# Prefix sums of four chunks as 64x64 tiles from three exact bf16 parts, with row 1's sums swapped between partition halves, and new orders of the whole program

## The chip, the cores and the metric

The kernel runs on one core of one Trainium2 chip. TensorE (PE) multiplies matrices into PSUM, VectorE (DVE) and ScalarE (ACT) work element by element, GpSimd (POOL) does slower element work and issues DMAs by software, and SyncE (SP) here only issues DMAs. Each engine takes its instructions strictly in order. The metric is the device time of one execution in microseconds. Before the change the median of three runs is 196.53 us (195.69 to 196.65).

## The reference

A gated linear attention is followed by a bilinear feed-forward layer. Batch 4, 8 heads, 768 positions, head size 48; the model width is 8 x 48 = 384 and the hidden width 1536.

```python
for t in range(S):
    state = alpha[:, :, t, :, None] * state + einsum('bhd,bhe->bhde', k[:, :, t], v[:, :, t])
    y[:, :, t] = einsum('bhd,bhde->bhe', q[:, :, t], state)
x = y.transpose(0, 2, 1, 3).reshape(B * S, H * D)
out = (x @ w_a) * (x @ w_b) @ w_out
```

The kernel does the recurrence in blocks. Within a block the decays are products of alpha, so it takes the logarithm of alpha, adds up along the positions (the prefix sums of this case), and scales q by exp(sum) and k by exp(-sum). Then masked scores q k^T times v give the part inside a block, and a state of 48x48 per head carries the rest over.

## The kernel before

**Chunks.** There are six chunks. Chunk c holds the two batch rows `2*(c%2)` and `2*(c%2)+1` (called u = 0 and 1 below, "row 0" and "row 1") and the 256 positions number c//2. A partition holds two successive positions, so 128 partitions hold 256 positions of a row. They are split at partition 64 into two halves (g = 0 and 1) of 128 positions each, and the prefix sums start anew in each half. Chunks 2, 3, 4, 5 are the ones that the change is about; chunk 0 sums every position by itself (`cum_both`, L588 and L589), and chunk 1 goes on as it was.

**The order.** Nothing is scheduled by the compiler: `PROGRAM` (L17 to L405) lists all operations of all chunks in one sequence, as `chunk: op args; op args`, and each engine gets its own instructions in that order. A number at the end of a PE operation is the PSUM bank (8 banks, L449). The letters V, S, P, Y at the end of others name VectorE, ScalarE, GpSimd and SyncE's DMA queue.

**One chunk.** `ld` loads alpha, k, q, v (L547). `ln` takes the logarithm (ACT, L554). `l2` adds the two positions of a partition (DVE, L561). The prefix sum is a product with an upper triangular matrix of ones, in which the block between the two halves is zero. The fast fp32 form of the product (type fp32r) rounds its input, so the sum to be multiplied is first split: `H` makes the rounded part `lh` (ACT L596 or DVE L598), `L` the remainder `ll` (DVE, L604), and `A2` multiplies both with the 128x128 triangle `utr`, two matmuls of 384 columns for one batch row (L628). `E` takes exp of plus and minus the sums (ACT, L656), `mk` and `mq` multiply k and q with them into `QKp` (DVE, L666); before that `lv` brings the first position of a pair to the level of the second (L642, on POOL or DVE; `ra` on ACT, L635, prepares a factor). `dr` and `dl` (SP, L671 and L676) carry the last sum of each half through DRAM into the column form `bl` that the state needs. `T` transposes `QKp` by DMA on SP (L718) in chunks 2 to 5; chunks 0 and 1 transpose on PE (`C`, L707, and `Ce`, L713 or L715) and take the decay from PE and ACT (`dk` L687, `de` L692).

**Attention and state.** `K` multiplies keys with values (L744), `k` updates the state (DVE, L758, L761, L762; it reads `bl`), `D` makes scores (L773), `M` or `Mc` then `Mm` masks them (L778; L782 on ACT and L786 on DVE), `SB`, `SA` and `Y` add up the output in PSUM (all L797), `X` takes it out as `xT` (L832, L834). `K`, `D`, `SB`, `SA`, `Y` use PE as four 64x64 tiles at once: four matmuls on different row and column halves of the array run side by side. In all of them the two row halves write different PSUM banks at any one time.

**Feed-forward.** `a` and `b` multiply `xT` with a 128-column piece of w_a and w_b (three matmuls each, L851; 512 columns for `*`, 256 for one row), `as` copies a (ACT, L857), `pr` multiplies (DVE, L865), `o` and `oc` are the last product (six matmuls of 384 or 192 columns, L873 and L884), `ot` takes it out (L888, L890), `st` stores it (SP, L906). All of these use the array whole, 128x128. In `PROGRAM` the feed-forward of a chunk is spread between the attention steps of the next ones, and so PE has work while the other engines prepare.

**The start.** `fill 7 6` (L571) runs seven matmuls on zeros while the first alpha is loaded.

Of the kernel before, what the change touches and what calls it, by code (L numbers as in the profile page):

```python
# [17 lines left out]
0: ld a 0b Y; cm 0; cz 0 q P; cz 0 b P; c1; cs 0 m V; c1a; ld a 0a Y; ld k 0b Y; ld q 0b Y; cu; ld q 0a Y; fill 7 6; cu2 P; ld v 0 P; cus; ld a 1 P; ln 0b  # L18
0: B 0b 5; ln 0a; ci; ld q 1 P; B 0a 0; E 0b i; E 0b b; ld k 0a Y; cz 1 b P; ld k 1 P; dk 0 3; mk 0b V; mq 0b V; E 0a b; C 0 1 4; cm 1; ld v 1 P; E 0a i
0: mq 0a V; W b 0 256; fill 3 1; mk 0a V; Ce 0 1 S; C 0 0 0; v 0 V; de 0; D 0 1 6; Ce 0 0 V; K 0 0 5; k 0 0 V; W a 0 256; M 0 1; D 0 0 4; SB 0 0; ln 1; W a 256 768  # L20
0: cz 0 v V; W b 256 768; M 0 0; B 1a 2
1: ld a 0 P
0: cs 1 0 P
1: ld a 1 P
0: B 1b 6; E 1a i; E 1a b; mq 1a V; mk 1a V; W a 768 1536; dk 1 5; E 1b i; C 1 0 2; de 1; v 1 S; mk 1b V; SA 0; Y 0; Ce 1 0 V; W b 768 1536; D 1 0 3
1: ld k 0 P
0: E 1b b; K 1 0 5; cs 1 m V; mq 1b V; X 0 S
1: ld v 0 P
0: K 0 1 2; C 1 1 6; a 0 0 0; a 1 0 7; Mc 1 0; k 0 1 V; Ce 1 1 V; k 1 0 V; a 2 0 3; as 1 0
1: ld q 0 P  # L30
0: cs 0 0 P; b 1 0 1; D 1 1 6; as 0 0; SB 1 4; Mm 1 0 V; as 2 0; Mc 1 1; a 3 0 0; pr 1 0; a 4 0 2; c2 P; Wo 0 6; cz 1 q V; Wo 6 12; b 2 0 3; pr 2 0; Mm 1 1 V
0: as 3 0; b 0 0 6; b 4 0 1; b 5 0 7; pr 0 0; Y 1; SA 1; K 1 1 6
1: ln 0
0: as 4 0
1: l2 0 V; ld k 1 P
0: X 1 S; b 3 0 0; a 5 0 2
1: ln 1
0: a 5 1 4; a 4 1 5; pr 3 0; pr 4 0; as 5 0; a 3 1 0; b 5 1 3
1: l2 1 V
0: pr 5 0; as 4 1; b 4 1 2; as 5 1; a 1 1 5; b 1 1 1; pr 4 1  # L40
1: ld q 1 P
0: cz 1 v P
2: ld a * P
0: as 1 1; a 6 * 4; as 3 1; pr 1 1
1: ra 0
0: a 0 1 0; a 2 1 7; a 8 * 1; b 3 1 2; pr 5 1; k 1 1 V
1: H 1 V; H 0 S
0: as 6 *
1: L 1 V
0: b 2 1 3; a 11 * 5; pr 3 1  # L50
1: L 0 V
0: a 7 * 6
1: ld v 1 P
0: as 11 *; b 6 * 2; as 2 1; pr 6 *; b 11 * 7; a 10 * 4
1: ra 1
0: as 0 1; pr 2 1
1: v 0 V
0: pr 11 *; as 7 *
1: lv 0 k P; A2 0 2
2: ld k * P  # L60
0: b 0 1 0
1: A2 1 5
0: as 8 *; b 7 * 3
1: lv 0 q V
0: pr 0 1
2: ld q * P
1: E 1 i; E 0 b
0: pr 7 *
1: E 1 b; E 0 i; mq 0 V
0: b 10 * 6; b 9 * 1; a 9 * 7; as 9 *; as 10 *  # L70
1: mk 0 V
0: b 8 * 0
1: dk * 5
0: pr 8 *; pr 10 *; pr 9 *
1: C 0 1 3; C 0 0 4
0: o 3 0 0
1: Ce 0 1 S; de *; Ce 0 0 V; K 0 0 7; D 0 0 4; k 0 0 V; K 0 1 3; D 0 1 1; Mc 0 0; lv 1 k P; SB 0 6; M 0 1
0: o 3 1 -
1: mk 1 V
0: o 0 0 5; ot 3 S  # L80
2: ln *
1: lv 1 q V
2: ld v * P
3: ld a * P
0: o 0 1 -
1: mq 1 V
0: o 2 0 4
1: Mm 0 0 V; k 0 1 V; C 1 0 2
0: o 1 0 0
1: Ce 1 0 V; v 1 V  # L90
2: l2 * V
0: ot 0 S; o 1 1 -
2: ra 0
1: SA 0
0: ot 1 S
2: H * S
1: D 1 0 1; K 1 0 3
2: lv 0 k P
1: M 1 0; Y 0
0: o 2 1 -  # L100
1: X 0 S; C 1 1 5
0: ot 2 S
1: a 5 0 6
2: L * V
1: Ce 1 1 V
2: lv 1 k P
1: a 3 0 1; k 1 0 V; as 3 0; a 1 0 0; as 5 0; b 1 0 7; b 3 0 2; as 1 0
2: A2 1 1
1: pr 3 0
2: ra 1  # L110
3: ld k * P
1: pr 1 0; SB 1 5
2: E 1 i
1: D 1 1 3; K 1 1 2; M 1 1
2: lv 1 q P; lv 0 q P; E 1 b
1: a 11 0 0
2: A2 0 7
1: as 11 0; b 11 0 1
2: E 0 i
1: b 5 0 0; pr 11 0  # L120
2: E 0 b
1: a 4 0 4; pr 5 0; a 0 0 3
2: dr
1: a 6 0 1; k 1 1 V; as 4 0; as 0 0; a 2 0 0; b 4 0 7
2: mk 1 V
1: as 6 0; b 6 0 3; pr 6 0; a 7 0 1; b 0 0 2; pr 4 0; b 7 0 4; pr 0 0; a 9 0 3; as 9 0
2: mq 1 V
1: as 2 0; SA 1; Y 1; as 7 0
2: T 1
1: b 9 0 2; X 1 S; pr 7 0; a 8 0 3; pr 9 0; b 2 0 0; as 8 0  # L130
2: v 1 S
1: b 8 0 1; pr 2 0; a 10 0 4; b 10 0 2
3: lv 0 k P
1: a 0 1 0
2: mq 0 V
1: as 10 0; a 9 1 5; as 0 1; pr 10 0; a 5 1 6
4: ld a * P
1: b 5 1 7
3: ln *
1: b 0 1 3; pr 8 0; a 2 1 0  # L140
2: dl
3: lv 1 k P
1: as 5 1; pr 0 1; a 1 1 2; b 1 1 4; as 1 1; pr 5 1; as 9 1; b 9 1 3; pr 1 1; as 2 1; a 8 1 6
2: mk 0 V
1: a 4 1 7; b 2 1 1
2: v 0 S
1: as 4 1; pr 9 1; a 11 1 2; b 11 1 0; b 4 1 5; pr 2 1; b 8 1 3; pr 4 1; as 8 1; pr 8 1
3: l2 * V
1: a 3 1 4
2: T 0  # L150
1: as 11 1; a 7 1 1; b 3 1 6
0: st 3 Y
1: o 2 0 5; a 10 1 7; as 7 1
3: ld q * Y
1: pr 11 1; as 3 1
0: st 1 Y
1: as 10 1; pr 3 1
2: D 1 0 3; K * 0 1; Mc 1 0; D 1 1 6; k * 0 V
1: a 6 1 0; b 7 1 2
3: ra 1  # L160
2: Mc 1 1
1: pr 7 1
5: ld a * Y
1: b 10 1 3; o 2 1 -; as 6 1
3: ra 0
0: st 0 Y
1: b 6 1 4; ot 2 S; pr 10 1
2: Mm 1 0 V; D 0 0 2; K * 1 1
3: H * V
1: pr 6 1; o 3 0 0  # L170
2: Mc 0 0; k * 1 V; Mm 1 1 V; SB 0 4; SB 1 6
3: L * V
2: D 0 1 2
3: lv 1 q P
1: o 0 0 1
2: Mc 0 1
1: o 3 1 -
2: Mm 0 0 V
4: ln *
3: A2 1 3  # L180
2: Mm 0 1 V; SA 1
3: ld v * P
4: ld v * P
2: Y 1; Y 0; X 1 V; SA 0
3: A2 0 2
2: X 0 S
3: E 0 b
1: o 0 1 -
3: lv 0 q V; E 1 b; E 0 i; mk 0 V
1: ot 3 S  # L190
3: E 1 i
2: b 5 * 6; b 3 * 4; a 4 * 5; a 5 * 7
1: ot 0 S
3: mq 1 V
2: a 3 * 2; a 2 * 1
3: dr
2: a 1 * 3; as 5 *; b 0 * 7; as 3 *; b 1 * 0; as 1 *
3: v 1 V
2: pr 5 *; pr 3 *; as 2 *
1: st 0 Y; st 3 Y  # L200
4: ld q * P
3: dl
2: b 2 * 3
3: mq 0 V
2: a 6 * 1
3: T 0
0: st 2 Y
2: as 6 *; pr 1 *
4: l2 * V; H * V; ra 1
2: as 4 *; b 4 * 2; a 11 * 0; b 6 * 6; a 0 * 4; b 8 * 1  # L210
1: o 1 0 5
4: L * V
2: pr 2 *; pr 6 *
3: v 0 V
2: as 0 *; a 8 * 3; pr 4 *; as 11 *; pr 0 *
3: mk 1 V
2: b 11 * 2; a 7 * 6; as 8 *; pr 11 *
1: o 1 1 -
2: pr 8 *
3: T 1  # L220
1: st 2 Y
3: K * 0 2
1: ot 1 S
3: k * 0 V
4: ld k * Y
1: st 1 Y
3: K * 1 0; D 0 0 3
2: as 7 *
3: Mc 0 0
2: b 9 * 1  # L230
3: k * 1 V
2: a 9 * 7
5: ld k * Y
2: b 10 * 5; as 9 *; a 10 * 6; b 7 * 3; pr 9 *; as 10 *; o 0 0 0; pr 7 *; pr 10 *
3: D 1 1 6; D 1 0 1
4: lv 1 k P
3: M 1 1
2: o 0 1 -
3: Mc 1 0
5: ld q * P  # L240
3: Mm 1 0 V; SB 0 3
2: ot 0 S
3: SB 1 1; D 0 1 5
4: lv 1 q V; A2 0 0
2: o 2 0 7
3: Mc 0 1
4: ra 0; lv 0 k V
5: ln *
4: E 0 b
3: Mm 0 1 V  # L250
2: o 3 0 6
3: Mm 0 0 V
5: lv 1 k P
4: lv 0 q P
5: ld v * P
3: Y 1; SA 0; Y 0; SA 1
2: o 3 1 -
3: X 0 S; X 1 V
2: o 2 1 -
4: mq 0 V; A2 1 2  # L260
2: ot 2 S
3: a 2 * 5
5: l2 * V
3: b 4 * 3
4: E 1 b; E 0 i; E 1 i
3: b 3 * 4; a 4 * 7; b 2 * 2
4: v 1 S
3: as 2 *
4: dr
5: H * S  # L270
2: ot 3 S
5: ra 0
2: st 0 Y
4: mk 0 V
3: as 4 *
4: mk 1 V
2: st 2 Y
3: a 8 * 1
4: T 0
3: a 1 * 0; a 0 * 6; b 8 * 7; as 8 *; b 5 * 5; pr 2 *; pr 4 *  # L280
4: v 0 V; dl
5: lv 0 q V
3: pr 8 *
4: mq 1 V
5: lv 0 k V
3: as 0 *
5: ra 1
3: a 3 * 1; a 5 * 3; b 0 * 7; a 9 * 6; as 5 *; pr 5 *; a 7 * 3; a 11 * 5; pr 0 *; as 9 *; as 3 *; as 1 *
4: T 1
3: b 9 * 6; b 1 * 1  # L290
5: lv 1 q V
3: pr 9 *; a 6 * 2; pr 3 *; as 11 *; pr 1 *; as 6 *
4: K * 0 0; D 0 0 4
5: L * V
3: as 7 *; b 11 * 6; b 6 * 7; pr 11 *; a 10 * 1; pr 6 *
4: Mc 0 0
2: o 1 0 5
3: as 10 *
4: k * 0 V; D 1 0 3; D 1 1 6; D 0 1 1
5: v 1 S  # L300
4: Mc 1 0; M 1 1
5: A2 0 0
2: o 1 1 -
4: SB 0 6; Mc 0 1; Mm 0 0 V; SB 1 3
2: ot 1 V
5: A2 1 2
3: b 7 * 1
5: E 1 i; E 1 b; E 0 b
3: b 10 * 5
4: Mm 0 1 V; Mm 1 0 V  # L310
3: pr 7 *; o 1 0 2
5: mk 1 V
3: pr 10 *; o 2 0 1
5: mq 1 V
4: Y 1; SA 0
5: dr
2: st 3 Y
5: T 1
4: Y 0; SA 1; X 1 S
5: E 0 i  # L320
3: o 1 1 -; o 2 1 -
4: X 0 V
5: mk 0 V; mq 0 V
3: ot 1 S
4: a 6 * 0; a 7 * 5; as 6 *
5: T 0
4: b 6 * 3; as 7 *; a 1 * 6
5: dl
4: pr 6 *; a 0 * 5; b 7 * 7; pr 7 *
3: ot 2 V; st 1 Y  # L330
4: as 0 *; as 1 *; a 5 * 3; b 1 * 4; b 0 * 2
2: st 1 Y
3: st 2 Y
4: pr 1 *; as 5 *; pr 0 *
5: v 0 V
4: a 3 * 0; a 4 * 7; as 3 *
5: D 0 0 5
4: as 4 *
5: K * 0 4; M 0 0; D 1 1 2; D 1 0 0; Mc 1 1
3: o 3 0 7  # L340
5: k * 0 V; Mc 1 0
3: o 3 1 -
5: SB 1 5
3: ot 3 S
5: SB 0 3; D 0 1 0
4: b 10 * 2
3: o 0 0 7
5: M 0 1; Mm 1 0 V; Mm 1 1 V
4: b 3 * 1; b 4 * 0
3: o 0 1 -  # L350
4: pr 4 *; b 5 * 0
3: ot 0 S
5: SA 1
4: pr 5 *
5: Y 1; Y 0
4: pr 3 *
5: X 1 V; SA 0
4: a 2 * 7; a 10 * 6
5: X 0 S
4: as 10 *; as 2 *; a 8 * 5  # L360
5: a 4 * 3
4: b 2 * 0
3: st 0 Y
5: a 2 * 4
4: pr 2 *; as 8 *; a 9 * 7
5: b 2 * 1; a 11 * 0
4: pr 10 *; b 8 * 5
5: as 2 *; as 4 *; a 1 * 4
4: b 9 * 2; pr 8 *
5: pr 2 *; b 5 * 3; b 1 * 6  # L370
4: as 9 *
5: b 4 * 1; a 8 * 5
4: a 11 * 7
5: pr 4 *
4: pr 9 *
5: b 11 * 1; as 11 *; as 1 *; a 5 * 4; a 0 * 2; pr 11 *; pr 1 *; as 0 *; as 5 *; b 0 * 0; b 7 * 6
4: o 0 0 1; as 11 *
5: pr 5 *; pr 0 *; as 8 *; a 10 * 2
4: b 11 * 4
# [644 lines left out]
```

## Time and profile before

| what | value |
|---|---|
| median of 3 runs | 196.53 us (195.69 to 196.65) |
| the profiled execution: its own time | 196.2 us |
| its span (first to last instruction) | 194.4 us |
| PE / DVE / ACT / POOL busy | 189.4 / 133.2 / 106.4 / 50.6 us |
| prefix sums of chunks 1 to 5 on PE (L628) | 20 matmuls of 128x384, mean 446 and 336 ns |
| `L` on DVE (L604), 128x768 | 4, mean 1126 ns |
| `H` 128x768 on ACT (L596) / DVE (L598) | 2 of 854 ns / 2 of 557 ns |
| issues on SP | 10 loads, 8 transposes, 8 + 8 decay DMAs, 24 stores |

"Busy" counts an instruction from start to modelled end, and successive matmuls overlap: a 384-column matmul is shown with 326 ns where one follows the other every 162 ns. So what an operation costs PE is read from the chain of waits, whose pieces are cut from start to start and add up to the span.

### The profile page before, as it was taken

To read this page: it belongs to the slowest core of one execution; us is meant where nothing else is said; L and a number is where in the kernel's file an instruction comes from. 1 tells how busy PE (TensorE), PEld (TensorE's weight loads), DVE (VectorE), ACT (ScalarE), POOL (GpSimd) and SP (SyncE) were. 2 spreads that over 40 slices of the span, in tenths; PEclk is the share of its full clock that TensorE was granted. 3 is DMA by queue.
4 is the path that set the end of the run, shared out by engine and by line. 5 is a ranking of instruction groups with operands and counts; after the bars stand their busy time and mean duration, and the time that the engine had idled before them with its cause. 6 is when DMAs were issued, how large, how long until landed. Compare 5 with 4: busy or idle time off the path is not lost.

```text
span 194.4 us, 5977 instructions
## 1 busy us (share of the span) xinstructions
PE 189.4 (97%) x2582; PEld 119.6 (62%) x2582; DVE 133.2 (69%) x221; ACT 106.4 (55%) x197; POOL 50.6 (26%) x69
## 2 busy tenths in 40 slices
PE   7999999999999999999999999999999999999993
PEld 3988875566888876644557544557455644445562
DVE  2498777988998879579786777996585525543311
ACT  4458784655859777645547684863462253431311
POOL 8999749160727004400004500000000000000000
PEclk9999999999999999999999999999999999999999
DMA  5999999999976999998699599007850100000342
GB/s 145 270 210 220 244 240 229 261 254 263 246 199 113 189 200 303 141 281 165 113 291 231 82 205 146 1 3 72 177 138 0 44 3 0 0 0 0 129 146 95
DMA packets 57034, 29.40 MB, mean 151 GB/s; under 512 B 47560, under 2 KB 54600, under 8 KB 57008
## 3 DMA queue, kind: packets, MB, share of 16 engines
q0 software_dynamic: 19056, 15.73, 44.0%
q1 hardware_dynamic: 37808, 13.19, 32.3%
q8 instruction: 20, 0.33, 0.7%
q10 hardware_dynamic: 144, 0.10, 0.2%
q14 instruction: 6, 0.05, 0.1%
HBM read 25.98 MB, written 4.74 MB: 158 GB/s over the span
## 4 chain that ended last, share of the span: by engine, by line
PE 96%; DVE 1%; issue 1%; ACT 0%; DVEq 0%
PE psum L851 48%; PE psum L873 24%; PE psum L797 7%; PE psum L773 3%; PE psum L744 2%; PE psum L628 2%; PE psum L707 2%; PE psum L571 2%; PE psum L588 2%; PE psum L589 2%; PE psum L687 1%; PE psum L884 1%; DVE kqT L715 0%; DVE m L786 0%; DVE prod L865 0%
## 5 line engine op out<-in xcount | busy, mean ns | idle before, releaser
L851 PE MATMUL psum<-xT,wb_t 128*128 128x512 bf16 (+1 forms) x270 | 56.0, 337 | 0.0
L851 PE MATMUL psum<-xT,wa_t 128*128 128x512 bf16 (+1 forms) x270 | 55.5, 337 | 0.0
L873 PE MATMUL psum<-wo_t,prod 128*128 128x384 bf16 x276 | 49.5, 326 | 0.0
L851 PEld LDWEIGHTS <-wa_t 128*128 128x128 bf16 x270 | 25.9, 98 | 19.6 <-issue 0.2
L851 PEld LDWEIGHTS <-wb_t 128*128 128x128 bf16 x270 | 25.7, 98 | 19.9 <-issue 0.6
L873 PEld LDWEIGHTS <-prod 128*128 128x128 bf16 x276 | 26.0, 98 | 18.2 <-issue 0.5
L888 ACT ACTIVATE ot<-psum 128x384 f32<-128x384 f32 (+1 forms) x20 | 9.5, 480 | 20.4 <-PE psum L873 16.1
L642 POOL TENSOR_TENSOR k_t<-k_t,a_t 128x384 f32<-128x384 f32 x8 | 8.5, 1069 | 38.7 <-DMA k_t<-in_k_dram 36.0
L782 ACT ACTIVATE m<-psum 128x1024 bf16<-128x1024 f32 x15 | 15.1, 1022 | 4.3 <-PE psum L773 4.3
L778 DVE TENSOR_TENSOR m<-psum,mask 128x1024 bf16<-128x1024 f32 x9 | 11.0, 1217 | 3.4 <-PE psum L773 3.3
L832 ACT ACTIVATE xT<-psum 128x768 bf16<-128x768 f32 x8 | 6.5, 810 | 9.6 <-PE psum L797 9.5
L554 ACT ACTIVATE la<-a_t 128x1536 f32<-128x1536 f32 (+2 forms) x9 | 9.5, 1054 | 3.5 <-DMA a_t<-in_alpha_dram 3.4
L786 DVE TENSOR_TENSOR m<-m,mask 128x1024 bf16<-128x1024 bf16 x15 | 11.2, 765 | 0.1
L666 DVE TENSOR_TENSOR QKp<-k_t,invb 128x768 bf16<-128x768 f32 x10 | 9.4, 951 | 2.3 <-issue 1.5
L797 PE MATMUL psum<-m,vx 64*64 64x128 bf16 x576 | 10.3, 217 | 0.2 <-DVE m L786 0.2
L773 PE MATMUL psum<-kqT 64*64 64x128 bf16 x384 | 10.0, 219 | 0.3 <-DVE Sm L758 0.2
L666 DVE TENSOR_TENSOR QKp<-q_t,beta 128x768 bf16<-128x768 f32 x10 | 9.7, 972 | 0.2
L797 PEld LDWEIGHTS <-vx 64*64 64x64 bf16 x576 | 9.0, 107 | 1.0 <-issue 0.8
L547 POOL DMA_DIRECT2D v_t<-in_v_dram x8 | 8.4, 1053 | 0.1
L773 PEld LDWEIGHTS <-kqT 64*64 64x64 bf16 x384 | 6.9, 106 | 2.4 <-issue 2.0
L797 PE MATMUL psum<-kqT,Sm 64*64 64x128 bf16 x144 | 7.9, 220 | 0.0
L642 POOL TENSOR_TENSOR q_t<-q_t,ra 128x384 f32<-128x384 f32 x4 | 4.1, 1024 | 14.1 <-DMA q_t<-in_q_dram 12.8
(262 smaller groups left out, 286.2 us busy)
## 6 DMA issues: line engine op xcount, KB each, us to landing
out_dram<-ot SPq DMA_DIRECT2D x23, 192.0 KB, 2.9
a_t<-in_alpha_dram POOLq DMA_DIRECT2D x3, 768.0 KB, 13.9
q_t<-in_q_dram POOLq DMA_DIRECT2D x3, 768.0 KB, 9.2
k_t<-in_k_dram POOLq DMA_DIRECT2D x2, 768.0 KB, 12.1
v_t<-in_v_dram POOLq DMA_DIRECT2D x4, 384.0 KB, 7.1
k_t<-in_k_dram SPq DMA_DIRECT2D x2, 768.0 KB, 6.6
a_t<-in_alpha_dram POOLq DMA_DIRECT2D x3, 384.0 KB, 8.9
q_t<-in_q_dram POOLq DMA_DIRECT2D x3, 384.0 KB, 13.5
```

Source lines behind the costliest of these rows:

```text
L547: eng.dma_start(out=t[:, us, hs].rearrange("p b h r d -> p (b h) (r d)"), in_=src[ch.b0 + us.start:ch.b0 + us.stop, hs, ch.s * 2 * C:(ch.s ...
L554: nc.scalar.activation(out=ch.la[:, us, hs].rearrange("p b h r d -> p (b h r d)"), in_=ch.a[:, us, hs].rearrange("p b h r d -> p (b h r d) ...
L642: eng.tensor_mul(x, x, by)
L666: eng.tensor_mul(QKp[ch.c % 2][:, u, j, :, hs, :D], src[:, u, hs].rearrange("p h r d -> p r h d"), f)
L773: nc.tensor.matmul(s2[g * HC:(g + 1) * HC, r, p, rk, :], lhsT=ch.kqT[u][rs, 1, rk, 2 * h + p, g * HC:(g + 1) * HC], rhs=queriesT(ch, u, 2 ...
L778: nc.vector.tensor_mul(m.rearrange("p r a k s -> p (r a) (k s)"), ch.s2[u, h].rearrange("p r a k s -> p (r a) (k s)"), maskn(4))
L782: nc.scalar.activation(out=m.rearrange("p r a k s -> p (r a) (k s)"), in_=ch.s2[u, h].rearrange("p r a k s -> p (r a) (k s)"), func=AF.Copy)
L786: eng.tensor_mul(x, x, maskn(4))
L797: nc.tensor.matmul(y[c * DP:(c + 1) * DP, g, j // 2 * C:(j // 2 + 1) * C], lhsT=lhsT, rhs=rhs, start=(g, c) not in begun, stop=False, skip ...
L851: nc.tensor.matmul(p, lhsT=(wa_t, wb_t)[w][:, kk, f * 128:(f + 1) * 128], rhs=ch.xT[:, kk, us, :], start=(kk == 0), stop=(kk == KT - 1))
L873: nc.tensor.matmul(op, lhsT=ch.prod[:, f, at:at + C], rhs=wo_t[:, f, :], start=(f == 0), stop=(f == NFF - 1))
L888: nc.scalar.activation(out=o_, in_=i_, func=AF.Copy)
```

## The change

1. **Four chunks sum differently.** After `l2`, `sw` on SP copies row 1's sums into a third slot of `l2` with the partition halves swapped (two DMAs of 64 partitions x 384 fp32). `R 0` and `R 1` (DVE, 128x768 each) replace `H` and `L`: the upper 16 bits of an fp32 read as bf16 are its truncated value, so `R 0` subtracts them from the sum, `R 1` subtracts the upper 16 bits of that remainder, and the upper 16 bits of the three stages together are the exact sum. `AQ` multiplies the three parts (every second bf16 in memory) with a 64x64 bf16 triangle: 3 parts x 2 rows x 2 halves = 12 matmuls of 384 columns on 64x64 tiles. Thanks to the swap the two rows and two halves stand on the four different tiles. Row 0's sums go to one bank, row 1's to the next; in a bank, the two halves of a row come from the two row halves of the array. Both rows are summed by one operation, where there were two `A2`.
2. `c3` makes the bf16 triangle `utb` on DVE, once.
3. **New orders.** The whole `PROGRAM` is written anew: the positions of almost all operations, their banks, and who does some of them. Counted over the program: `fill` 10 to 8 matmuls (7 to 5 at the start); `Ce` one from DVE to ACT; one `M` less, one `Mc` and `Mm` more; `ot` 18 on ACT and 5 on DVE become 15 and 8; `v` 5 ACT and 7 DVE become 4 and 8; loads 25 POOL and 10 SP become 22 and 13; the early memsets change engines. The feed-forward, score and output operations are as many as before.
4. `bls`, `dr` and `dl` get another layout (batch row first), with as many DMAs as before. `apart` replaces the test for chunk 0 and changes no operation.

```diff
-0: ld a 0b Y; cm 0; cz 0 q P; cz 0 b P; c1; cs 0 m V; c1a; ld a 0a Y; ld k 0b Y; ld q 0b Y; cu; ld q 0a Y; fill 7 6; cu2 P; ld v 0 P; cus; ld a 1 P; ln 0b
+0: cz 0 q V; cs 0 m P; ld a 0b Y; c1; c1a; cs 0 0 P; cz 0 v V; ld a 0a Y; ln 0b; cu; fill 5 2; ld k 0b Y; ld q 0b Y; cu2 P; cus; cm 0; cz 1 q V; B 0b 0; ld q 0a Y
...
+2: lv 0 k P; l2 * V
+1: Ce 1 0 S; Y 0; K 1 0 5; K 1 1 6
+2: sw Y
+1: k 1 0 V; SA 0; D 1 0 3; X 0 S
+0: o 2 0 5
+1: k 1 1 V
+0: ot 3 S; ot 1 V
+2: ra 0
+1: M 1 0; a 3 0 1; a 1 0 2; as 3 0; as 1 0; b 1 0 0
+2: ra 1
+1: a 11 0 7; b 3 0 6
+3: ld a * P
+1: a 5 0 2
+0: o 2 1 -
+1: pr 1 0; as 5 0
+2: R 0
+1: D 1 1 3; pr 3 0
+2: lv 1 k P; R 1
+0: ot 2 S
+1: b 5 0 2; b 11 0 0; b 4 0 6; pr 5 0; a 4 0 1; Mc 1 1; as 11 0; Mm 1 1 V
+2: v 0 V; AQ 4
...
-5: A2 0 0
-2: o 1 1 -
-4: SB 0 6; Mc 0 1; Mm 0 0 V; SB 1 3
-2: ot 1 V
-5: A2 1 2
...
+4: SB 0 4
+5: AQ 0; E 0 i; E 0 b; E 1 b
+3: o 1 0 2; b 7 * 3
+5: dr
...
+    def const_utb(eng):
+        ENG[eng].tensor_copy(utb, ut)
...
+    def top(t):
+        return t.bitcast(BF16).rearrange("p b h (d t) -> p b (h d) t", t=2)[:, :, :, 1]
+
+    def rest(ch, n):
+        name = ("lh", "ll")[n]
+        t = wk.tile([C, 2, H, D], F32R, name=name, bufs=1)
+        setattr(ch, name, t)
+        x, hi = (ch.l2[:, 0::2], top(ch.l2)[:, 0::2]) if n == 0 else (ch.lh.bitcast(F32), top(ch.lh))
+        nc.vector.tensor_sub(t.bitcast(F32).rearrange("p b h d -> p b (h d)"), x.rearrange("p b h d -> p b (h d)"), hi)
...
-        for t in (ch.lh, ch.ll):
+        for n, x in enumerate((top(ch.l2)[:, 0::2], top(ch.lh), top(ch.ll))):
             for u in range(2):
                 for g in range(2):
                     gs, to = slice(g * HC, (g + 1) * HC), slice((g ^ u) * HC, ((g ^ u) + 1) * HC)
-                    nc.tensor.matmul(p[to, u], lhsT=utr[gs, gs], rhs=t[gs, u].rearrange("p h d -> p (h d)"), start=(t is ch.lh), stop=(t is ch.ll))
+                    nc.tensor.matmul(p[to, u], lhsT=utb[gs, gs], rhs=x[gs, u], start=(n == 0), stop=(n == 2))
...
-    bls = [cst.tile([C, B, P2], F32, name=f"bl{i}") for i in range(2)]
+    bls = [cst.tile([C, 2, 2, P2], F32, name=f"bl{i}") for i in range(2)]
```

`sw` calls a function that the kernel before had and did not use:

```python
def cross(ch, eng):
    for g in range(2):
        eng.dma_start(out=ch.l2[(1 - g) * HC:(2 - g) * HC, 2].rearrange("p h d -> p (h d)"),
                      in_=ch.l2[g * HC:(g + 1) * HC, 1].rearrange("p h d -> p (h d)"))
```

## The prediction

> **What bounds the kernel now.** I read the busy shares first, then the chain of waits (whose pieces are cut from start to start and add up to the span), then groups by form for the prices of single operations, and last the tiles that DMAs carry.
>
> ```profile
> PE 189.4 (97%) x2582; PEld 119.6 (62%) x2582; DVE 133.2 (69%) x221; ACT 106.4 (55%) x197; POOL 50.6 (26%) x69
> ```
>
> ```profile
> PE 96%; DVE 1%; issue 1%; ACT 0%; DVEq 0%
> ```
>
> PE is busy 97% of the span and is 96% of the chain that ends last. So time is won or lost in two ways only: by what PE must execute, and by waits that make it idle. DVE at 69% and ACT at 55% have room. Next, pieces of the chain (start, length, what):
>
> ```profile
> 1.19 3.17 PE psum L571 x7
> 4.36 0.75 PE psum L588 x2
> 5.10 0.64 PE psum L589 x2
> ...
> 6.79 0.33 PE psum L588 x2
> ...
> 72.23 0.35 PE psum L773 x16
> 72.58 0.50 PE psum L744 x32
> 73.08 1.08 PE psum L873 x6
> 74.16 0.46 PE psum L797 x24
> 74.62 0.22 PE psum L773 x16
> 74.84 2.06 PE psum L873 x12
> 76.90 0.35 PE psum L628 x2
> 77.25 1.80 PE psum L797 x120
> 79.05 0.55 PE psum L628 x2
> 79.59 0.99 PE psum L873 x6
> 80.58 10.36 PE psum L851 x48
> ```
>
> Here are the prices. Sixteen 64x64 matmuls of 128 columns (L773) take 0.22 us, so four side by side take 55 ns. They take 0.35 when they come right behind a full-array product: entering the tile form costs 0.13. An output product (six matmuls, L873) takes 0.99 before another full-array operation and 1.08 before a tile operation: another 0.09. A round trip through the tile form costs 0.22. `A2` (L628) takes 0.35 behind a full-array operation and 0.55 behind a tile operation.
>
> ```profile
> L604 DVE TENSOR_TENSOR ll<-l,lh 128x768 fp32r<-128x768 f32 x4 | 4.5, 1126 | 0.0
> L561 DVE TENSOR_TENSOR l<-la 128x768 f32<-128x768 f32 x4 | 3.8, 950 | 0.0
> ```
>
> The chain's first lines are the start: B's pairs (L588, L589) take 0.64 at first and 0.33 from 6.79 on; the change falls at about 6.4, some 5.2 us behind the first matmul at 1.19.
>
> **1. Eight `A2` go.** Their chain pieces are 0.35, 0.35, 0.35, 0.55 (chunk 2 and 3 up to 79 us), 0.54, 0.35, 0.55 and 0.54: 3.58 us. In four of them some 0.1 is the price of leaving the tile form, which the next operation pays instead. Saved: 3.2.
>
> **2. Four `AQ` come.** Three parts, each four tiles of 384 columns: three waves x (3 x 55 ns) = 0.50 us, times four = 2.0. The trace has no 384-column tile and no tile group whose two row halves write one bank. The bounds: 2.0 if the four tiles run side by side, as in all the rows above; 4.0 if the two halves of a batch row go one after the other; 8.4 if all twelve matmuls do (12 x 0.175, half a fast `A2`, times four). The last I leave out of the range: the two column halves of a row half run side by side in every tile row of the trace, and nothing here changes that. I take 2.0, since 16 matmuls in 0.22 is the nearest row. 1 and 2 give -1.2. The Trainium skill ("TensorEngine Tiling (Array Packing)", Gotcha 1: PSUM Pressure) speaks against it: different row tiles cannot access the same PSUM bank at once; by it the sum of this step would be +0.8 instead of -1.2, and no run here shows it yet.
>
> **3. The order.** Read in PROGRAM's sequence, full-array work is broken by a group of tile operations 23 times before and 28 times after. The `AQ`s stand next to other tile operations and add none. Five round trips x 0.22 = +1.1. Bounds: 0 (the entries coincide with waits that are there anyway) and 1.1.
>
> **4. The start.** Two fills fewer. B waits for the logarithm (3.46 to 3.98) in both, and before it starts at 4.15. After, a DVE memset stands ahead of the fill's zeros, about 0.5 us, so five fills of 0.43 run from about 1.6 to 3.75 and PE idles some 0.4 us: directly 0, because the logarithm decides.
>
> ```profile
> 3.46 0.52 ACT L554 ACTIVATE la<-a_t 128x384 f32<-128x384 f32 x1 [1.44 <-DMA a_t<-in_alpha_dram]
> ```
>
> Chunk 0's mask half moves on POOL behind more DMA issues; `M 0 1` may be up to 0.5 late, on DVE, where the first `Y` wants it only later. The wait before `Y 1` goes, since the new order masks chunk 0 earlier: -0.2 (bounds -0.4 and +0.3, the 0.3 if the late mask reaches PE).
>
> ```profile
> L797 PE MATMUL psum<-m,vx 64*64 64x128 bf16 x576 | 10.3, 217 | 0.2 <-DVE m L786 0.2
> ```
>
> **5. DVE and ACT.** `R 0` and `R 1`, eight 128x768 subtractions like L561: 8 x 0.95 = 7.6. Gone: `L` 4 x 1.126 = 4.5 and two `H` on DVE, 1.1. DVE +2.0; ACT loses two `H`, 1.7. `c3` some 0.2 on DVE. DVE goes from 69% to about 71%: 0 on the path, hidden by the feed-forward matmuls between a chunk's sums and its use. If that cover is gone, the `AQ` waits by those 2.0 / 4 = 0.5 each.
>
> **6. The swap.** Eight DMAs more on SP, each between `l2` and `R 0`. The nearest DMAs are those of the decay rows, also from SBUF on SP:
>
> ```profile
> DMA to landing us min/median/max: 2.6/3.0/4.4
> ```
>
> With the second issued some 0.3 behind the first, the last lands 2.9 to 4.7 behind `l2`. For chunk 2, DVE has between `l2` and `R 0` two state updates (0.35 + 0.71), an `ot` 0.55, an `M` 1.22 and a `pr` 0.44 = 3.3 us, and PE's work beyond. By the median, no wait; by the maximum, 1.4. Behind the waiting `R 0` on DVE stand `pr 3 0`, `R 1`, `pr 5 0`; these free the banks that PE's `b` wants, so a wait here reaches PE. Chunks 3 to 5 have over 2 us of other work on top. I take 0; above, the transposes' landing times under load (next fence) in place of the rows' would make it 3.
>
> SP also issues three more loads, so a `T` may start later. Transposes land so:
>
> ```profile
> DMA to landing us min/median/max: 4.8/6.1/7.2
> ```
>
> In chunk 5, PE has between `AQ` and `D 0 0` 13 feed-forward pieces x 0.648 (10.36/16) = 8.4, four output products 3.9, and two `SA` and `Y` some 2.0: 14.3 us, against exp and multiplications (about 6) and a transpose of at most 7.2: about 1 us to spare. 0. `dr`, `dl`: as many as before, 0. The tail ends with the same output half, evacuation and store: 0.
>
> **Sum.** -1.2 + 1.1 - 0.2 = -0.3. The profiled execution took 196.2 (194.4 of it the span), so 195.9; it stands 0.33 under the median of 196.53, so 196.2 as a median.
>
> **The rivals.**
> *The banks collide.* Slower by one mechanism: the two halves of a batch row write one bank from both row halves of the array, and the pairs take turns. Place: inside each `AQ`; price 4 x 0.5 = +2.0, giving 198.2. It decides from about half of that price on. For it: every tile operation of before keeps the row halves in different banks at any one time, so no row proves it harmless. Against: at any one partition the two writes go to different banks here too. This is also the case in which the change does not do what it says, four tiles at once.
> *The clock comes late.* The slow passes ended 5.2 us after the first matmul. If the new gap of 0.4 us before B, and the start at 1.6 in place of 1.2, put that off by one more stretch of this length, the four remaining pairs of B run at 0.64 in place of 0.33: 4 x 0.31 = +1.3, giving 197.5. Against: gaps of that size later in the trace left durations as they were. The Trainium skill ("TensorE: Matmul & The Clock Gate", Part 1: The HAM clock gate) says that full speed follows a sustained busy window of about 3.4 us that runs free of the kernel's start; the slow passes here, 5.2 us, agree with a window missed in part, and by it the +1.3 would be a matter of the phase.
> *A DMA is late.* Swap or chunk 5's transpose, by 1 to 3 us on PE: 197.2 to 199.2. For: margins of 0 to 1 us. Against: the medians fit.
> *The gain is larger.* The five extra entries cost nothing, as they stand where PE waits or drains anyway: -1.1, giving 195.1, and 194.9 with the better end of the start. For: the pieces of 0.02 to 0.03 us between L797 and L773 show switches between tile groups to be free. Against: all entries from the full array that I priced cost.
>
> **How the numbers follow.** A measurement of this kernel can tell about 0.5% (1 us: the runs spread from 195.69 to 196.65) from no change. My forecast 0.42, own range 195.2 to 197.3 (same 0.34, faster 0.06, slower 0.02); banks 0.17, all slower; clock 0.14 (slower 0.11, same 0.03); DMA 0.10 (slower 0.08, same 0.02); larger gain 0.17, all faster. Together: faster 0.23, same 0.39, slower 0.38. The range goes from 194.9, the larger gain with the better start, to 198.5, the banks with the worse start (198.2 + 0.3); left out are the late DMA's upper half, collisions of several and unforeseen gains.
>
> **What will show it.** In the profile after, L628's successor as tiles: an `AQ` of about 0.5 us in the chain (1.0 if the banks collide); PE's busy time down by 1 at most; the number of `L773` and `L797` groups in the chain up by five, each first one at 0.35; B's pairs at 0.33 from the fifth on; no idle time of `R 0` on DVE that names the swap, or under 1 us; no PE wait on `kqT` late in the span. The prediction is wrong if PE shows idle time of over 1 us at any place of the middle: I found none that the new order must make, but I summed margins from medians, and one DMA later than these breaks it.

## The result, and the profile after

The changed kernel takes 196.77 us (median of 16 runs, 196.3 to 197.74) where the kernel before, run beside it, takes 195.76 us (16 runs, 195.22 to 196.65). The ratio is 1.0051, with a 95% interval of 1.0034 to 1.0067: about 1.0 us slower. The forecast was 196.2 and "no change": the time lies in the range, the direction was missed. That the time lies in the range is partly luck: the forecast stood on a median before of 196.53 us from three runs, and 16 runs give 195.76. Each against its own median before, the forecast was 0.3 us faster and the result is 1.0 us slower. The profiled execution after took 196.63 us, its span 194.9.

The page of the changed kernel, busy time of PE and the shares of the chain by engine:

```profile
PE 188.1 (97%) x2612; PEld 117.9 (60%) x2612; DVE 133.5 (69%) x224; ACT 106.7 (55%) x195; POOL 48.6 (25%) x67
PE 90%; DMA 5%; DVE 2%; ACT 0%; issue 0%; SPq 0%; DVEq 0%
```

PE has 1.3 us less to do than before (189.4), and yet the span is longer. The chain no longer runs through PE alone: 5% of it are DMAs. One of them stands in the middle. The chain of waits of the changed kernel between 46 and 57 us (start, length, what):

```profile
46.53 0.88 DVE l L556
...
48.08 5.95 DMA l<-l
...
54.12 0.96 DVE lh L614
55.08 0.36 DVE prod L869
...
55.48 0.81 PE psum L855 x6
56.30 0.63 PE psum L624 x11
```

That is chunk 2: `l2` makes the sums, SP issues the swap, its second half lands 5.95 us after its issue, `R 0` and then a feed-forward product run on DVE, and PE goes on at 55.48. The same place in the timeline of DVE, with the idle time before an instruction in brackets:

```profile
54.12 0.96 DVE L614 TENSOR_TENSOR lh<-l 128x768 f32<-128x768 f32 x1 [1.83 <-DMA l<-l]
54.99 0.43 DVE L869 TENSOR_TENSOR prod<-as__1077,psum 128x256 bf16<-128x256 bf16 x1
```

`R 0` waits 1.83 us, `pr 3 0` stands behind it in order, and PE's next `b` wants the bank which that product frees. The table of PE's waits, after (engine, line, what it waited for, us in total, times, longest):

```profile
PE psum L566 <- DVE og L465: 1.7, 1, 1.7
PE psum L855 <- DVE prod L869: 1.1, 1, 1.1
PE psum L801 <- DVE Sm L762: 0.6, 1, 0.6
PE psum L583 <- ACT la L548: 0.3, 1, 0.3
```

and before:

```profile
PE psum L571 <- DVE og L475: 1.2, 1, 1.2
PE psum L773 <- DVE Sm L758: 0.2, 1, 0.2
PE psum L797 <- DVE m L786: 0.2, 1, 0.2
```

The 1.1 us are that wait; before, PE had no wait for a feed-forward product. The first line of each is the start: the first matmul comes at 1.7 us, where it came at 1.2.

Now the price of `AQ`, from the chain of the changed kernel, chunks 3 and 5:

```profile
79.52 0.51 PE psum L624 x12
...
129.30 0.51 PE psum L624 x12
```

Twelve matmuls in 0.51 us, as four side by side should take. The tiles run at once; the banks do not collide. These two stand behind other tile operations. In chunks 2 and 4 `AQ` comes behind full-array work and takes 0.63 us (one and two of its matmuls are missing from the record).

A single profile has a start of its own (below), so I compare stretches that leave it out: from the end of the second take-out `xT` of chunk 0 to the start of the last matmul. Before: 24.92 to 190.87, 165.96 us (165.99 in a second profile of it). After: 24.71 to 191.53, 166.82. So 0.86 us are lost behind the start. PE is idle for 0.08 us of the stretch before and for 1.16 us of it after. The new order puts two more feed-forward matmuls of 256 columns into the stretch (184 for 182), about 0.2 us, so between the two orders a stretch is good to that much only; between kernels of one order it holds the same work.

### The profile page after: what moved, and what is told of

The parts are those of the page before. It is cut to its first block, busy times and chain, and to the rows that moved or that the text cites. A ratio compares the mean times of both kernels' runs of the same rounds, so it can differ in the third digit from the quotient of the medians.

```text
span 194.9 us, 6070 instructions
## 1 busy us (share of the span) xinstructions
PE 188.1 (97%) x2612; PEld 117.9 (60%) x2612; DVE 133.5 (69%) x224; ACT 106.7 (55%) x195; POOL 48.6 (25%) x67
## 4 chain that ended last, share of the span: by engine, by line
PE 90%; DMA 5%; DVE 2%; ACT 0%; issue 0%; SPq 0%; DVEq 0%
PE psum L855 47%; PE psum L877 22%; PE psum L801 7%; PE psum L777 3%; DMA l<-l 3%; PE psum L748 2%; PE psum L711 2%; PE psum L583 2%; DMA a_t<-in_alpha_dram 1%; PE psum L584 1%; PE psum L691 1%; PE psum L624 1%; PE psum L888 1%; DVE kqT L719 1%; DVE lh L614 0%; DVE l L556 0%
## 5 line engine op out<-in xcount | busy, mean ns | idle before, releaser
L643 POOL TENSOR_TENSOR q_t<-q_t,ra 128x384 f32<-128x384 f32 x6 | 7.1, 1188 | 50.5 <-ACT xT L836 28.5
L786 ACT ACTIVATE m<-psum 128x1024 bf16<-128x1024 f32 x16 | 15.9, 1022 | 5.3 <-PE psum L777 5.2
L892 ACT ACTIVATE ot<-psum 128x384 f32<-128x384 f32 (+1 forms) x17 | 7.9, 472 | 15.9 <-PE psum L877 12.7
L782 DVE TENSOR_TENSOR m<-psum,mask 128x1024 bf16<-128x1024 f32 x8 | 9.8, 1221 | 2.7 <-PE psum L777 2.0
L790 DVE TENSOR_TENSOR m<-m,mask 128x1024 bf16<-128x1024 bf16 x16 | 10.5, 685 | 1.3 <-ACT m L786 1.3
L836 ACT ACTIVATE xT<-psum 128x768 bf16<-128x768 f32 x9 | 7.2, 810 | 6.1 <-PE psum L801 5.8
L894 DVE COPY ot<-psum 128x384 f32<-128x384 f32 x8 | 4.4, 550 | 8.7 <-PE psum L877 8.7
L669 DVE TENSOR_TENSOR QKp<-k_t,invb 128x768 bf16<-128x768 f32 x10 | 10.2, 1031 | 0.0
L643 POOL TENSOR_TENSOR k_t<-k_t,a_t 128x384 f32<-128x384 f32 x6 | 7.2, 1194 | 9.1 <-DMA k_t<-in_k_dram 9.1
```

The lines of the kernel that those rows point to most:

```text
L643: eng.tensor_mul(x, x, by)
L669: eng.tensor_mul(QKp[ch.c % 2][:, u, j, :, hs, :D], src[:, u, hs].rearrange("p h r d -> p r h d"), f)
L782: nc.vector.tensor_mul(m.rearrange("p r a k s -> p (r a) (k s)"), ch.s2[u, h].rearrange("p r a k s -> p (r a) (k s)"), maskn(4))
L786: nc.scalar.activation(out=m.rearrange("p r a k s -> p (r a) (k s)"), in_=ch.s2[u, h].rearrange("p r a k s -> p (r a) (k s)"), func=AF.Copy)
L790: eng.tensor_mul(x, x, maskn(4))
L892: nc.scalar.activation(out=o_, in_=i_, func=AF.Copy)
```

## The experiments

All ratios are to the kernel before, run beside the changed one on the same chip; 0.001 is 0.2 us. Where two ratios are compared, both intervals count: such a difference is uncertain by 0.4 to 0.7 us.

**Is it the wait for the swap?** In `rest` and `cum_quads` the swapped slot is not read:

```diff
-        x, hi = (ch.l2[:, 0::2], top(ch.l2)[:, 0::2]) if n == 0 else ...
+        x, hi = (ch.l2[:, 0:2], top(ch.l2)[:, 0:2]) if n == 0 else ...
-        for n, x in enumerate((top(ch.l2)[:, 0::2], top(ch.lh), top(ch.ll))):
+        for n, x in enumerate((top(ch.l2)[:, 0:2], top(ch.lh), top(ch.ll))):
```

> The changed kernel, in which R and AQ read row 1's sums from where l2 put them and not from the swapped copy. The swap's DMAs are still issued, but nothing waits for them. (Left out: row 1's sums of chunks 2 to 5 then belong to the other partition half, so that row's output is not the reference's.) Theory, the late swap: in the profile after, R 0 of chunk 2 sat 1.8 us until the swap landed, and PE sat 1.1 us behind pr, with two delays of 0.2 more beside it; without the wait the time falls by 1.3 us, from 196.8 to about 195.5, 0.998 to 0.999 of before, and no matmul of the feed-forward waits on DVE. Rival, the new order: the loss is made by tile form entries and waits elsewhere, and the wait only moves; then 196.5 or more, 1.004 and up.

Measured: ratio 0.9986 (0.9961 to 1.0012), 0.0065 or 1.27 us under the changed kernel, as the late swap would have it. The stretch behind the start falls to 165.57. PE's waits:

```profile
PE psum L566 <- DVE og L465: 1.7, 1, 1.7
PE psum L801 <- DVE Sm L762: 0.6, 1, 0.6
PE psum L691 <- DVE prod L869: 0.2, 1, 0.2
```

The wait on `prod` in the middle is gone (the 0.2 that is left belongs to chunk 1's decays). Without this one wait the whole change would be worth -0.0014 or -0.3 us, which is the sum I had predicted; but the interval reaches from -0.8 to +0.2 us.

**What are the new order and the new sums worth by themselves?** The new order with the old sums:

```diff
-2: sw Y
...
-2: R 0
+2: H * V
...
-2: lv 1 k P; R 1
+2: lv 1 k P; L * V
...
-2: v 0 V; AQ 4
+2: v 0 V; A2 0 4; A2 1 5
```

and the same in chunks 3, 4 and 5.

> The changed kernel with the old sums in the new order: no sw, H on DVE in the place of R 0, L in the place of R 1, two A2 in the place of each AQ. Theory, the late swap with the ledger of PE: A2 costs 1.5 us more than AQ over the program, the wait for the swap (1.3) goes: about 197.0, 1.005 to 1.008 of before, with no idle PE at 55 us; so exact sums and their wait cancel, and the new order as such is 1.1 to 1.3 slower than the old. Rival, the sums are at fault and the order is not: then this is back at before, 195.8, within 0.3.

Measured: 1.0044 (1.0023 to 1.0066), +0.86 us, just under what was expected, with an interval that reaches into it; the stretch is 166.43, 0.47 above before. The new order with its start, not the sums, makes this kernel slower than before. It has 29 groups of tile operations and not 28, since chunk 3's two `A2` cut a group that `AQ` leaves whole. Only 22 of them, against 19 before, lie in the stretch; the others come ahead of 25 us. Against e1_unswapped, the four `AQ` in place of eight `A2` are worth 0.0058 or 1.1 us in time (0.86 in the stretch), somewhat less than the 1.5 that I had worked out here from the pieces of the chain (3.58 less 4 x 0.51).

**Is it chunk 2 alone?** The same replacement in chunk 2 only.

> The changed kernel (new order), in which chunk 2 alone has H, L and two A2 instead of the swap, R and AQ. Theory, chunk 2's swap is the only one that PE waits for (1.3 us) and its AQ saves 0.38: 0.9 us faster than the changed kernel, 0.9995 to 1.0020 of before. Rival, the swaps of chunks 3 to 5 cost as well: 1.003 or more.

Measured: 1.0016 (0.9998 to 1.0034), stretch 165.83. This is within what was expected: PE has no wait that leads back to the swaps of chunks 3 to 5, and giving chunk 2 its `AQ` was a loss of some 0.7 us (0.0035). The three `AQ` that are left gain 0.0028 or 0.55 us on e2_old_sums (0.60 in the stretch), less than the 1.1 that 0.38 for each would make.

**Why does the swap land so late?** Three loads that are under way beside it are issued later.

```diff
-2: ld v * P
...
-2: ld q * P
...
-3: ld a * P
...
 2: lv 1 k P
+3: ld a * P
+2: ld v * P
+2: ld q * P
```

> The changed kernel, in which three loads on POOL (q and v of chunk 2, alpha of chunk 3) are issued behind lv 1 k, so that the loads' queue is nearly empty while chunk 2's swap is under way. They come late for chunk 2 and the time gets worse; only the swap is looked at. Theory, the loads share the DMA engines with the swap: its second half lands 2.6 to 3.5 us after its issue instead of 5.95, and R 0 waits for it less than 0.3 us. Rival, a copy from SBUF to SBUF of 64 rows of 1536 bytes is slow by itself: 5 us or more again.

In the changed kernel, the DMA view of 47.4 to 54.1 us, the swap's time (queue, packets, MB, share of the 16 engines' time):

```profile
q0 software_dynamic: 1009, 1.50, 99.8%
q1 hardware_dynamic: 160, 0.20, 11.9%
```

The loads of the software queue fill the engines while the swap is on its way. With those loads behind it, `R 0` reads so:

```profile
52.70 0.96 DVE L606 TENSOR_TENSOR lh<-l 128x768 f32<-128x768 f32 x1 [0.35 <-DMA l<-l]
```

The second half of the swap landed 3.87 us after its issue instead of 5.95, the first after 2.11 instead of 6.18, and `R 0` waited 0.35 instead of 1.83. (The 3.87 and the 0.35 lie a little outside what I had written; the loads began again at 51.7, before its last packets.) The software queue had 18.9% of the engines from 48.1 to 52.6 us, the time of this swap. The kernel as such took 199.75 us, since q and v now came late. So the load of the queue is the cause of most of the landing time. The profile of e1_unswapped, where the swap is issued though nothing waits for it, fits between: chunk 2's halves landed after 4.54 and 4.32 us, with the software queue at 78.2% from 48.7 to 53.6. In the changed kernel the first half of chunk 4's swap, with no packets of the software queue beside it from 82.3 to 85.0 us, took 2.69. The share alone does not set the landing: chunk 5's halves took 4.80 and 5.07 with the software queue at 146.1% from 111.2 to 116.8 us, in packets of 0.2 KB on average (3535 for 0.67 MB) where those beside chunk 2's swap have 1.5 KB.

**Can the swap be started earlier?**

```diff
 1: C 1 1 4; Ce 1 1 V
+2: l2 * V
 0: o 3 1 -; ot 0 V
...
-2: R 0
 1: D 1 1 3; pr 3 0
+2: R 0
```

> The changed kernel with two moves for chunk 2: l2 stands ahead of the evacuation ot 0 and of v 1 on DVE, so that the swap starts about 1 us earlier, and R 0 stands behind pr 3 0, so that this product does not wait for the swap. The output is the reference's. Theory, the late swap: nearly the whole wait goes, and 195.5 to 195.8 comes out, 0.997 to 1.000 of before. Rival, load: the swap lands at the same time as before because the loads in front of it set its landing; then only pr 3 0's share is won, 0.3 to 0.5, 196.3 or more.

Measured: 1.0022 (1.0008 to 1.0035), 0.0029 or 0.6 us better than the changed kernel, between the two: neither expectation fits, though the time is near the rival's; for its reason the landing would have had to stay where it was. The swap was issued at 46.67 and 47.26, 0.8 earlier, and landed 0.7 earlier; the copy still took 6 us:

```profile
47.26 6.07 DMA l<-l
...
53.43 0.97 DVE lh L608
```

`R 0` still waited 1.26 us. In this profile PE reached chunk 3's `AQ` at 78.44 instead of 79.52, but then waited 0.71 us inside it, which the profile puts down to a mask product on DVE; the stretch is 166.91, no better than that of the changed kernel. So the gain of 0.6 us (0.2 to 1.0) stands on the ratio alone.

**What does a cut of a tile group cost?** Eight full-array operations are moved one place, ahead of the last operation of a neighbouring tile group, for instance:

```diff
-4: a 10 * 3
 ...
 5: D 0 1 0
+4: a 10 * 3
 5: SB 1 6; SB 0 4
```

> The changed kernel, in which eight full-array operations are moved ahead of the last operation of the tile group in front of or behind them, so that a group is cut in two: 36 groups of tile operations instead of 28, nothing else changed. Theory, my price of 0.22 us for a round trip through the tile form: +1.8 over the changed kernel, 198.4 to 198.7, 1.013 to 1.016 of before. Rival, the entries coincide with drains and waits that are paid anyway: +0.5 at most, 197.3 or less.

Measured: 1.0169 (1.0147 to 1.0191), 2.3 us over the changed kernel: more than the 1.8 of the theory, whose range the interval still touches, and far more than the rival's 0.5. Cuts ahead of 55 us also move chunk 2's swap and its wait, so I repeated it on the kernel without swap.

> The kernel of e2_old_sums (new order, old sums, no swap that could get worse) with the same eight cuts of tile groups as in e5_more_groups. Theory, 0.22 us for each round trip through the tile form: 1.8 us over e2_old_sums, which stood at 1.0044: 1.0125 to 1.0145. Rival, the 2.3 us of e5_more_groups were all entries, 0.29 each: 1.0155 to 1.0175. Rival, the entries are free: 1.006 or less.

Measured: 1.0215 (1.0182 to 1.0249), 3.4 us over e2_old_sums. Outside all three expectations, and the profile shows one reason:

```profile
108.81 0.45 PE L630 MATMUL psum<-lh,utr 128*128 128x384 f32 x1 [1.25 <-DVE m L783]
```

One cut put chunk 4's first `A2` behind a mask product, a wait of 1.25 that the uncut order hides. The cuts themselves can be read from the chain. Uncut, e2_old_sums, scores, cross terms, and later the block of `SA` and `Y` of chunk 5:

```profile
147.54 0.35 PE psum L767 x16
147.88 0.34 PE psum L791 x24
...
153.57 1.80 PE psum L791 x120
```

Cut, e8_groups_old_sums, the same matmuls with one feed-forward piece (L856) between them:

```profile
149.88 0.35 PE psum L778 x16
150.23 0.75 PE psum L856 x3
150.98 0.46 PE psum L802 x24
...
156.79 0.29 PE psum L802 x12
157.09 0.75 PE psum L856 x3
157.84 1.63 PE psum L802 x108
```

The feed-forward piece costs 0.75 instead of 0.65, and the tile operations are 0.12 longer in both (0.46 for 0.34; 0.29 + 1.63 for 1.80): 0.22 for a cut, twice. That is the price I had used. Eight cuts at 0.22 and the wait above make 3.0 of the 3.4; the last 0.4 I have not told apart.

**The sums alone in the old order.** Chunks 3 to 5 get `sw`, `R`, `AQ` in the `PROGRAM` of before, chunk 2 stays, 23 tile groups; for chunk 3:

```diff
 3: l2 * V
+3: sw Y
...
-3: H * V
+3: R 0
...
-3: L * V
+3: R 1
...
-3: A2 1 3
+3: AQ 2
...
-3: A2 0 2
```

> The order of before with the exact sums alone: chunks 3, 4 and 5 get sw, R 0, R 1 and one AQ each, chunk 2 keeps H, L and two A2 (its swap would fall among the loads). Besides these, l2 of chunk 3, T 0 of chunk 2 and mq 0 of chunk 4 move by up to four places, and three banks are renamed so that AQ finds two neighbours. 23 groups of tile operations as before. Theory, from the ledger of PE (A2 to AQ saves 1.5 us for four chunks, 0.38 a chunk, and the order costs the rest): 0.9 to 1.1 us faster than before, 0.9945 to 0.996, about 195.0. Rival, the sums bring nothing where they are not covered by their own order: DVE's 0.5 us more per chunk and the swap in SP's queue in front of the transposes cost what PE saves; then 0.999 to 1.003.

Measured: 1.0078 (1.0048 to 1.0109), slower. (In this kernel a feed-forward piece of chunk 4 uses the bank of one output tile of chunk 3 too early, so that tile's values are lost; the amount of work is the same.) The chain shows a new wait that my own edit made:

```profile
67.15 1.37 SPq L610
...
68.56 0.59 SPq L917
...
69.20 4.51 DMA kqT<-QKp
```

On SP the swap (L610) and a store (L917) now stood in front of `T 0` of chunk 2, which left at 69.2 instead of 65.4; PE waited 1.9 us. With that undone, and then without chunk 3's exact sums:

```diff
-3: sw Y
 2: T 0
+3: sw Y
```

> As e6_sums_old_order (the order of before, exact sums for chunks 3, 4 and 5), with the one fault that its trace showed taken out: there T 0 of chunk 2 stood on SP behind chunk 3's swap and a store, was issued 3.8 us later than before, and PE waited 1.9 us for it. Here T 0 stands where it was, the swap behind it, R 0 one product later (and one bank is renamed, a 6 of chunk 4). Theory: three chunks save 0.38 us each and no wait takes it back: 0.9940 to 0.9965 of before, about 0.7 to 1.2 us faster. Rival, DVE and SP have no room for R and the swap in this order either: 0.999 or more, with a wait of over 0.7 us on PE in the middle of the span.

> As e9_sums_3to5, but chunk 3 keeps H, L and its two A2; exact sums for chunks 4 and 5 only. Theory: two chunks save 0.76 us, 0.995 to 0.9975. Rival: no gain, 0.999 or more. If this one is faster than e9_sums_3to5, chunk 3's swap costs more than its 0.38.

Measured: 0.9992 (0.9972 to 1.0013) and 0.9991 (0.9972 to 1.0010). Neither is faster than before beyond its interval, and less than the 0.7 to 1.2 and 0.5 to 1.0 us that I expected. The stretches are 166.02 and 165.64. In the chain of e9_sums_3to5 chunk 3's `AQ` (L632) is followed by a gap to which the profile gives no cause:

```profile
76.42 0.64 PE psum L632 x12
77.06 0.67 PE psum L809 x44
77.73 0.55 issue
```

> e9_sums_3to5 once more, for a second profile: in the first one PE stood 0.55 us at 77.7 us (in Y 1 of chunk 2) with nothing named that it waited for, and 0.4 us ahead of chunk 1's first A2. Theory, the order makes these gaps: both are there again, at the same operations, within 0.15 us. Rival, they are chance (the phase at which this execution ran): at least one is absent, and PE's time from the first dk to the last matmul falls from 183.4 to under 183.0.

In the second profile the gap is there at the same operation, but shorter:

```profile
77.28 0.63 PE psum L632 x10
77.91 0.67 PE psum L809 x33
78.58 0.21 issue
```

The stretch is 165.75. Some matmul records are missing in this profile, so PE's time from the first `dk` on could not be added up. This gap is at least partly chance. The other, ahead of chunk 1's first `A2`, is not. In the chain of e9_sums_3to5 it reads

```profile
32.45 0.09 issue
32.54 0.59 PE psum L637 x2
```

and before

```profile
33.26 0.34 PE psum L628 x2
```

so 0.34 us more, and it is 0.34 more in e12_again (0.09 and 0.59), e10_sums_4to5 (0.09 and 0.58) and e6_sums_old_order (0.09 and 0.59) too, while e13_before_again has 0.34 like the kernel before. The kernels with exact sums in the old order make this loss each time, in chunk 1, which the edit was not about; what causes it the profiles do not name. It explains much of the missing gain: the stretch of e10_sums_4to5 is 0.32 shorter than before, and with the 0.34 its gain would be 0.66, against the 0.76 expected of two chunks; in e9_sums_3to5, -0.06 with 0.34 and the gap of 0.55 makes 0.83, against 1.1 of three.

**The start.**

> The kernel before once more, for a second profile of its start. In the first one B's pairs were slow until 6.4 us; the profiles of the kernels that start like the changed one have the switch anywhere between 5.5 and 7.9 us. Theory, the phase of the clock is free of the kernel's start: the switch falls at another moment than 6.4, by up to 1.5 us either way, with the first matmul at 1.2 again. Rival, it follows the first matmul by a fixed 5.2 us: 6.3 to 6.5 again.

Slow passes ended at 6.29, as at 6.46 in the first profile. By this run alone, the fixed distance would stand. But e6, e9 and e10 have the same start, first matmul at 1.19, and there they ended at 4.96, 4.42 and 4.46. In the eight profiles with the start of the changed kernel (first matmul at 1.73) they ended at 5.16, 5.22, 5.42, 5.73, 5.79, 7.50, 7.80 and 7.85.

## Why the prediction was wrong, step by step

**The sum.** It came to -0.3 and the measurement to +1.0. The step that failed is 6, the swap: its wait stood in the sum as 0, by the median of the decay rows' landing, and the wait was worth 1.27 us (e1_unswapped; the two intervals together leave it uncertain by some 0.6). The last half landed 6.6 us behind the end of `l2` (47.41 to 54.03), where the step had 2.9 to 4.7. The cover was misread too, to the good: DVE was at work or waiting for PE for 4.9 us between `l2` and `R 0` (to 52.29) and not 3.3, or the wait would have been longer still. The prediction's own sign of being wrong came true: PE idle for over 1 us in the middle, and `R 0` waiting for the swap for 1.83. The queue behind the waiting instruction was named rightly: `R 0`, then `pr 3 0`, then PE's `b`. The nearest row was the wrong one to read: it was a median over chunks and a transfer of 3 KB, while in that window the loads fill the DMA engines. The row to be read was the landing time of the transposes under load (6.1), which I had only set beside it as "3".

**1 and 2, sums.** -1.2 predicted; 1.1 in time and 0.86 in the stretch between e1_unswapped and e2_old_sums. The eight `A2` of e2_old_sums are 3.17 us of its chain, the four `AQ` of the changed kernel 2.28 and not 2.0, since two of them are the first in their tile group and cost 0.63. The rival that banks collide (198.2) is out: 0.51 for twelve matmuls of 384 columns leaves no room for pairs in turn. The Trainium skill ("TensorEngine Tiling (Array Packing)", Gotcha 1: PSUM Pressure) states that different row tiles cannot access one bank at once; here both row halves write one bank, in different partitions, and take 0.51 us. The measurement decides.

**3, order.** The total fits: the traces have 28 groups against 23, and 0.22 a round trip was seen again in the cuts. The new order with old sums is 0.86 us slower (0.45 to 1.3), against +1.1 for steps 3 and 4 together with its 29th group. That the loss is made by the groups one by one is not shown: three groups more in the stretch should cost 0.66 us, and it is 0.47 longer, some 0.2 of it for unequal work. The rival "extra entries cost nothing" is out for the cuts; for the order's own entries it is unlikely.

**4, start.** The sign is not shown. The wait before `Y 1` is gone from the table of waits, but a wait of 0.6 for `Sm` stands in place of 0.2 + 0.2, and the first matmul is 0.54 us later. The rival "clock late" was half right: no fixed 1.3 us, but chance. The moment at which B's passes become fast lies between 4.4 and 7.9 us in fourteen profiles, on average at 5.5 with the old start (six) and 6.3 with the new (eight). That these averages differ by chance can't be excluded. What a lucky start gains is partly lost again: in e9 and e10 PE then waited for the alpha of chunk 0's row 1, which landed at 10.44 and 10.69 us. The granted clock of the profile reads 1.00 in the slow passes too (before from 4.1 to 6.4 us, after from 4.3 to 5.7), so these traces show that the passes are slow, not why.

**5, the transposes, the tail.** DVE's busy time rose by 0.3 us (133.2 to 133.5) and not by 2.0: the step counted the sums' operations alone, and the new order moves others as well. DVE's work behind `R` and the loads and transposes of chunks 3 to 5 cost nothing that I could find in the changed kernel, as predicted; e6_sums_old_order shows how near that was, with SP's queue.

**The chances.** The late DMA had 0.10, with 197.2 to 199.2. It was the case that came, with 1.3 of its "1 to 3 us"; that the time is under 197.2 all the same is due to the lower median before.

## What to carry to other kernels

Where a change puts a small DMA into a chain, read how full the DMA engines are in exactly that window, and which loads are in flight, instead of a median landing time of similar DMAs. Look then at what stands behind the instruction that waits for it: here a subtraction that nobody was in a hurry for held up a product on the same engine, and that held up PE. And a gain from cheaper matmuls has to be set against the tile groups and the entries that the order around it makes: the exact sums won about 1.1 us, the order that came with them lost about 0.9.

## What the runs showed of the hardware that I had not expected

- Half a swap, 64 rows of 1536 bytes within SBUF, landed 2.11 and 3.87 us after its issue where the loads' queue took 18.9% of the DMA engines (e7), 4.54 and 4.32 at 78.2% (e1) and 6.18 and 5.95 at 99.8%; in the one case with a larger share, 146.1% in smaller packets, it was 4.80 and 5.07. An earlier issue by 0.8 us brought its landing forward by 0.7, at the same 6 us.
- The moment at which PE becomes fast moves by 3.4 us from run to run (4.42 to 7.85) with the same or nearly the same start, and by 2.0 us in the six profiles with the same start (4.42 to 6.46). The Trainium skill ("TensorE: Matmul & The Clock Gate", Part 1: The HAM clock gate) describes a window of about 3.4 us that runs free of the kernel's start; the spread here is about as wide as that window, and wider than the 500 ns either way that the same section gives for the moment.
- Matmuls of two row halves that write the same bank in different partitions ran side by side: 0.51 us for three waves of 384 columns.
